# Thirteen gate/up units of a gated mix kernel as seven-product 2x2 blocks, with the operand sums and the normaliser work moved around them

## The chip, the cores and the metric

The kernel runs on one core of one Trainium2 chip. The metric is the device time of one execution in microseconds (us); it is compared by runs of both kernels on the same chip, in rounds. A single run on one core is called slow when it is over 1.5% above the fastest run of the same kernel.

Engines in the profile: PE is the matmul engine (TensorE), PEld its weight loads, DVE is VectorE, ACT ScalarE, POOL GpSimd, SP the engine that issues most DMAs.

## The reference, cut to what matters

```python
def _B_ref(x, w_gate, w_up, w_down):              # D = 640, F = 1728, S = 2048, bf16
    return (_gelu(x @ w_gate) * (x @ w_up)) @ w_down

g = _sigmoid((x * gate_w).sum(-1, keepdims=True))
a = _A_ref(x, A_wqkv, A_wo)                       # linear attention with 32 heads of 20
b = _B_ref(x, B_w_gate, B_w_up, B_w_down)
return g * a + (1 - g) * b
```

The attention part divides by a normaliser, `den` below; its input is also x.

## The kernel before

The 2048 tokens are worked in four quarters of 512. Per quarter there is a gate/up stage ("E"): 13 full f-tiles of 128 hidden columns and one half tile, which holds gate and up for the last 64 columns. A full f-tile is two groups of five matmuls of 512 columns, one group for gate and one for up. E of quarter q is followed by the output stage ("F") of quarter q-1, and the last quarter's F ends the kernel. Before all that, quarter 0 has its E stage and a stage "KQ" makes keys and queries. In the F stage a "join" is the DVE instruction that combines a finished PSUM bank with a stored partial result and so frees the bank.

The F stage already multiplies 2x2 blocks with 7 products in place of 8 (the Strassen-Winograd scheme), from sums of blocks that VectorE prepares ("S sums", `phase_S`, of tokens; "T sums", of weights). PSUM has eight banks, handed out in turn.

```python
    def ps_tile(name, hold=False):                 # eight banks, in turn
        b = bank_at[0] % NB
        ...
        return banks[:, b * QW : (b + 1) * QW]

    def e_mm(ps, w, ft, q, t0=0, tw=QW):           # QW = 512, ND = 5
        for dk in range(ND):
            nc.tensor.matmul(ps[:, t0 : t0 + tw], lhsT=w[:, dk, ft * P : (ft + 1) * P],
                             rhs=xT[q][:, dk, t0 : t0 + tw], start=(dk == 0), stop=(dk == ND - 1))

    def e_out(q, ft, psg, psu):
        gl = work.tile([P, QW], BF16, name="gl")
        nc.scalar.activation(out=gl[:], in_=psg[:], func=ACT.Gelu_apprx_tanh)
        nc.vector.scalar_tensor_tensor(out=hT_cur[q][:, ft, :], in0=psu[:], scalar=HS, in1=gl[:],
                                       op0=ALU.mult, op1=ALU.mult)

    def phase_E(q, ft):
        if ft < NF - 1:
            psg = ps_tile("ps_g")
            e_mm(psg, wg, ft, q)
            psu = ps_tile("ps_u")
            e_mm(psu, wu, ft, q)
            e_out(q, ft, psg, psu)
        ...                                        # the half tile
    ...
    side.update({                                  # what is queued behind which unit
        ...
        (2, 0): [(den_inv, 6), (den_out, 6, 7)],
        (2, 2): [(s_tiles, 1), (phase_S, 1, "h", 0)],
        (2, 3): [(phase_S, 1, "h", 1)],
        (2, 4): [(phase_S, 1, "p"), (phase_S, 1, "x")],
        (2, 5): [(den_mul, 8, 9)],
        (2, 7): [(den_inv, 8), (den_mul, 10, 11), (den_out, 8, 9)],
        ...
    })
    with tc.manual_schedule():                     # every engine runs in the order written
        for q in range(1, NQ):
            for ft in range(q == 1, NF):
                phase_E(q, ft)
                beside(q, ft)
            phase_F(q - 1)
        phase_F(NQ - 1)
```

`den_mul` (POOL) multiplies 640 columns, `den_inv` (DVE) reduces and inverts, `den_out` (POOL, then a transposing DMA) scales. `(2, 5)` means: in quarter 2 (the third), behind the unit at place 5. `("F", q, a)`, `("C", q, a)` and `("D", q, a)` are places in half a of the F stage of quarter q.

Of the kernel before, what the change touches and what calls it, by code (L numbers as in the profile page):

```python
# [8 lines left out]
ACT = mybir.ActivationFunctionType  # L9
ALU = mybir.AluOpType  # L10
# [6 lines left out]
def kernel(  # L17
# [48 lines left out]
    ov = ctx.enter_context(tc.tile_pool(name="ov", bufs=1))  # L66
    work = ctx.enter_context(tc.tile_pool(name="work", bufs=3))
    psum = ctx.enter_context(tc.tile_pool(name="psum", bufs=1, space=bass.MemoryType.PSUM))
    NB = 8
# [19 lines left out]
    x_sb = [x_all[:, 4 * q : 4 * q + 4, :] for q in range(NQ)]  # L89
    pk_q = [ov.tile([P, 4, D], BF16, name=f"pk{q}", tag="slab_a", bufs=NQ) for q in range(NQ)]  # L90
    pk = [pk_q[t // 4][:, t % 4, :] for t in range(NT)]
    WQK = 2 * D + 1
# [91 lines left out]
    def e_mm(ps, w, ft, q, t0=0, tw=QW):  # L184
# [3 lines that stand above are left out]
# [6 lines left out]

    def phase_E(q, ft):
        if ft < NF - 1:
            psg = ps_tile("ps_g")
            e_mm(psg, wg, ft, q)
            psu = ps_tile("ps_u")
            e_mm(psu, wu, ft, q)  # L200
            e_out(q, ft, psg, psu)
        else:
            pgu = ps_tile("ps_gu")
            e_mm(pgu, wgu, 0, q)
            gl = work.tile([P, QW], BF16, name="gl")
            nc.scalar.activation(out=gl[0:FL, :], in_=pgu[0:FL, :], func=ACT.Gelu_apprx_tanh)
            nc.vector.scalar_tensor_tensor(out=hT_cur[q][0:FL, ft, :], in0=pgu[FL:P, :], scalar=HS,
                                           in1=gl[0:FL, :], op0=ALU.mult, op1=ALU.mult)

    def h_twin(q):  # L210
# [95 lines left out]

    g_sb = ov.tile([P, ND, D], BF16, name="g_sb", tag="slab_g")

# [253 lines left out]

    def phase_S(q, part, a=None):
        lo, hi = PART[part]
        c0, c1 = (0, TW) if a is None else (a * P, a * P + P)

        def blk(i, k):
            return ktiles(part, k, hT_cur[q], pqT[q])[:, :, i * TW + c0 : i * TW + c1]

        s1, s2, s3, s4 = (SS[q, i][:, lo:hi, c0:c1] for i in range(1, 5))  # L570
        sums(s3, blk(0, 0), blk(1, 0), ALU.subtract)
        sums(s1, blk(1, 0), blk(1, 1), ALU.add)
        sums(s2, s1, blk(0, 0), ALU.subtract)
        sums(s4, blk(0, 1), s2, ALU.subtract)

    side = {}

    def beside(*key):
# [3 lines left out]
    def phase_F(q):  # L582
# [34 lines left out]
        for a in range(2):  # L617
# [30 lines left out]
            d = keep_slot("d")  # L648
            join(d[:], b22, 0, c2)
            beside("D", q, a)  # L650
            product(x, a, 3, 0, 0, 3, 0, 0, False, True)
# [27 lines left out]
    with tc.manual_schedule():  # L679
        for ft in range(3, NF):  # L680
            phase_E(0, ft)
            if ft in (8, 9, 10, 11):
                x_sums((3, 1, 2, 4)[ft - 8])
        g4 = [banks[:, b * QW : (b + 1) * QW] for b in (6, 7)]
        g_done = 0
# [37 lines left out]
    def t_tiles():  # L723
        TS[2] = ov.tile([P, KS, HALF], FP16, name="t2", tag="slab_e")

    def m_part(i):
        phase_M(((0, 0), (0, 1), (1, 0)) if i == 0 else ((1, 1), (2, 0), (2, 1)))
# [15 lines left out]
        (1, 11): [(phase_S, 0, "x", 0)],  # L743
        ("F", 0, 0): [(phase_S, 0, "h", 1)],
        ("D", 0, 0): [(phase_S, 0, "p", 1), (phase_S, 0, "x", 1)],
        ("F", 0, 1): [(den_mul, 4, 5)],
        ("D", 0, 1): [(den_inv, 4), (den_mul, 6, 7), (den_out, 4, 5)],
        (2, 0): [(den_inv, 6), (den_out, 6, 7)],
        (2, 2): [(s_tiles, 1), (phase_S, 1, "h", 0)],
        (2, 3): [(phase_S, 1, "h", 1)],  # L750
        (2, 4): [(phase_S, 1, "p"), (phase_S, 1, "x")],
        (2, 5): [(den_mul, 8, 9)],
        (2, 7): [(den_inv, 8), (den_mul, 10, 11), (den_out, 8, 9)],
        (2, 9): [(den_inv, 10), (den_out, 10, 11)],
        (3, 0): [(den_mul, 12, 13)],
        (3, 2): [(den_inv, 12), (den_mul, 14, 15), (den_out, 12, 13)],
        (3, 4): [(den_inv, 14), (den_out, 14, 15)],
        (3, 5): [(s_tiles, 2), (phase_S, 2, "h", 0)],
        (3, 6): [(phase_S, 2, "h", 1)],
        (3, 7): [(phase_S, 2, "p"), (phase_S, 2, "x")],  # L760
        ("F", 2, 0): [(s_tiles, 3), (phase_S, 3, "h", 0)],
        ("D", 2, 0): [(phase_S, 3, "p", 0)],
        ("F", 2, 1): [(phase_S, 3, "x", 0), (phase_S, 3, "h", 1)],
        ("D", 2, 1): [(phase_S, 3, "p", 1)],
        ("F", 3, 0): [(phase_S, 3, "x", 1)],
    })
    with tc.manual_schedule():
        for q in range(1, NQ):
            for ft in range(q == 1, NF):
                phase_E(q, ft)  # L770
                beside(q, ft)
            phase_F(q - 1)
        phase_F(NQ - 1)
# [27 lines left out]
```

## Time and profile before

| | before |
|---|---|
| time, first six runs | 265.31 us (265.06 to 265.51) |
| span of the profiled run | 263.8 us |
| PE / DVE / ACT / POOL busy | 98 / 70 / 36 / 19% |
| one plain gate/up unit on PE | 2.16 us |
| E stage of the third and fourth quarter | 29.14 us each |
| F stage | 17.87 us |

From the page of the kernel before: busy time of each engine, then the busy tenths of PE and its granted clock (tenths of full speed) in 40 equal slices of the span.

```profile
PE 259.1 (98%) x1587; PEld 144.9 (55%) x1587; DVE 184.7 (70%) x343; ACT 94.5 (36%) x187; POOL 50.2 (19%) x50
PE   8999999999999999999999999999999999999994
PEclk9999999999999999999999999999999999999999
```

From 11.8 us on, when the first loads have landed, PE never pauses, and its clock is never lowered. A busy PE can still hide waits, so the next view matters more: the chain of work that ended last, in order of time (start us, us, what). Five of its pieces, from the third quarter's E stage to the start of the fourth's; L186 is gate/up, L603 and L610 the F stage:

```profile
148.25 29.14 PE banks L186 x135
177.39 7.33 PE banks L603 x54
184.72 0.65 PE banks L610 x8
185.37 9.89 PE banks L603 x72
195.26 29.14 PE banks L186 x135
```

Each piece starts where the one before ends, and each is PE. 29.14 us / 135 = 0.2159 us a matmul: PE streams 512 columns after 512 columns and waits for nobody. So only less work on PE can shorten this stretch; this change takes the streamed columns.

What do the others do meanwhile? The table by stage of the kernel before (window, length, then busy time of PE, PEld, DVE, ACT, POOL, the granted clock, DMA share and GB/s), for the same two E stages:

```profile
148.25:177.40 29.15, 29.15 (x137) 13.23 (x136) 26.20 (x44) 7.77 (x13) 16.37 (x13) 1.00 0.21 46
195.30:224.40 29.10, 29.10 (x137) 13.24 (x136) 22.30 (x38) 7.76 (x13) 8.04 (x6) 1.00 0.15 34
```

ACT has room; DVE is at 90% in the third quarter. Part of that is not work but waiting: DVE and POOL hold each other up. In order of time, DVE first, then POOL (start us, us, engine, line, operation, what, shape):

```profile
156.49 1.76 DVE L61 TENSOR_TENSOR s_1_1577<-hb 128x768 f16<-128x768 bf16 x1
158.29 1.64 DVE L61 TENSOR_TENSOR s_2_1578<-s_1_1577,hb 128x768 f16<-128x768 f16 x1
159.96 0.56 DVE L61 TENSOR_TENSOR sp<-hb,s_2_1578 128x768 f16<-128x768 bf16 x1
156.11 3.40 POOL L510 TENSOR_TENSOR prod<-pq_91,zrep 128x640 f32<-128x640 bf16 x2
```

The same kind of sum of 768 columns takes 1.76 and 1.64 us while POOL multiplies, and 0.56 us once POOL has stopped. The Trainium skill says the same in "SBUF — State Buffer", § Who interferes with whom: a VectorE instruction with two SBUF inputs contends with a GpSimd instruction that reads SBUF, one with at most one SBUF input, outside what the page calls two-port modes, does not.

The cost of a matmul of about half width can be read from this kernel too. Groups of instructions, shapes kept apart (what, shape, count, busy us and mean ns, idle before):

```profile
L249 PEld LDWEIGHTS <-xT_86 128*128 128x128 bf16 x60 | 5.9, 98 | 5.3
L249 PE MATMUL banks<-wqk,xT_86 128*128 128x257 bf16 x20 | 2.9, 273 | 0.0
```

The 273 ns include the depth of the pipeline; the pace is the difference of starts. The chain has a KQ tile, ten 512- and five 257-column matmuls, at 2.71 us; ten at 0.216 us are 2.16, so the five take 0.55 us, 110 ns each. The weight load of 98 ns fits under that.

### The profile page before, as it was taken

The numbers are of one execution on the slowest core, as the hardware profiler recorded it, in microseconds if no ns is written. First come the engines' busy times: TensorE is split into PE (matmuls) and PEld (weight loads), VectorE is DVE, ScalarE is ACT, GpSimd is POOL, SyncE is SP. The second block draws the span as 40 slices with busy tenths as digits, with TensorE's granted clock in tenths as the row PEclk, the third lists the DMA queues.
The fourth block names the chain that finished last, engine by engine and source line by source line (L and its number), as shares of the span: only waits on it lengthen the run. The fifth ranks groups of instructions, "written<-read, shape, count | busy, mean of one in ns | idle before, by whom it ended". The sixth has DMA issues, their size and how long they took to land.

```text
span 263.8 us, 4180 instructions
## 1 busy us (share of the span) xinstructions
PE 259.1 (98%) x1587; PEld 144.9 (55%) x1587; DVE 184.7 (70%) x343; ACT 94.5 (36%) x187; POOL 50.2 (19%) x50
## 2 busy tenths in 40 slices
PE   8999999999999999999999999999999999999994
PEld 3644444555556775444567544446764444767672
DVE  0775358589889995799994889982335997676132
ACT  3688222744555234822321122223112222312110
POOL 5000000000000004684000761383001810000000
PEclk9999999999999999999999999999999999999999
DMA  7999999000000019125001050031110220011011
GB/s 228 291 301 267 210 320 249 6 0 2 0 0 2 0 35 316 51 71 107 0 0 52 13 135 3 0 65 39 50 50 2 50 50 0 2 50 41 13 50 50
DMA packets 34959, 20.91 MB, mean 79 GB/s; under 512 B 20732, under 2 KB 34940, under 8 KB 34940
## 3 DMA queue, kind: packets, MB, share of 16 engines
q1 hardware_dynamic: 34498, 20.16, 28.2%
q10 hardware_dynamic: 442, 0.49, 0.6%
q8 instruction: 12, 0.20, 0.3%
q14 instruction: 7, 0.06, 0.1%
HBM read 12.62 MB, written 2.62 MB: 58 GB/s over the span
## 4 chain that ended last, share of the span: by engine, by line
PE 94%; DMA 4%; DVE 0%; SPq 0%; issue 0%
PE banks L186 44%; PE banks L603 26%; PE banks L249 14%; PE banks L347 6%; DMA wqk<-in_A_wqkv_dram 3%; PE banks L338 2%; DMA x_all<-in_A_x_dram 1%; PE banks L610 1%; PE banks L478 0%; PE banks L447 0%; DVE o_out L629 0%; SPq L122 0%; PE banks L417 0%
## 5 line engine op out<-in xcount | busy, mean ns | idle before, releaser
L191 ACT ACTIVATE gl<-banks 128x512 bf16<-128x512 f32 x52 | 31.0, 598 | 74.6 <-PE banks L186 70.6
L186 PEld LDWEIGHTS <-wu 128*128 128x128 bf16 x260 | 25.4, 98 | 30.7
L186 PEld LDWEIGHTS <-wg 128*128 128x128 bf16 x260 | 25.2, 98 | 29.4 <-issue 0.5
L192 DVE SCALAR_TENSOR_TENSOR hT_148<-banks,gl 128x512 bf16<-128x512 f32 x26 | 17.4, 681 | 11.4 <-PE banks L186 10.2
L192 DVE SCALAR_TENSOR_TENSOR hb<-banks,gl 128x512 bf16<-128x512 f32 x26 | 17.4, 677 | 10.9 <-PE banks L186 8.7
L266 ACT ACTIVATE phi<-banks 128x512 bf16<-128x512 f32 (+1 forms) x36 | 18.7, 526 | 15.5 <-ACT eneg L267 6.3
L510 POOL TENSOR_TENSOR prod<-pq_89,zrep 128x640 f32<-128x640 bf16 x2 | 2.8, 1408 | 95.0 <-ACT zrep L418 95.0
L625 ACT ACTIVATE m_all<-banks,omg_s 128x320 f32<-128x320 f32 x16 | 8.4, 528 | 27.2 <-PE banks L603 27.2
L629 DVE SCALAR_TENSOR_TENSOR o_out<-banks,omg_s,m_all 128x320 bf16<-128x320 f32 x24 | 12.2, 542 | 5.9 <-PE banks L603 5.9
L186 PE MATMUL banks<-xT_86,wg 128*128 128x512 bf16 x65 | 16.2, 379 | 0.0
L186 PE MATMUL banks<-xT_87,wg 128*128 128x512 bf16 x65 | 16.2, 379 | 0.0
L186 PE MATMUL banks<-xT_85,wg 128*128 128x512 bf16 x65 | 16.1, 379 | 0.0
L186 PE MATMUL banks<-xT_85,wu 128*128 128x512 bf16 x65 | 16.1, 379 | 0.0
L186 PE MATMUL banks<-xT_86,wu 128*128 128x512 bf16 x65 | 16.1, 379 | 0.0
L186 PE MATMUL banks<-xT_87,wu 128*128 128x512 bf16 x65 | 16.1, 379 | 0.0
L186 PE MATMUL banks<-xT_88,wg 128*128 128x512 bf16 x65 | 16.1, 379 | 0.0
L186 PE MATMUL banks<-xT_88,wu 128*128 128x512 bf16 x65 | 16.1, 379 | 0.0
L629 DVE SCALAR_TENSOR_TENSOR m_all<-banks,omg_s,m_all 128x320 f32<-128x320 f32 x8 | 4.4, 551 | 14.6 <-PE banks L603 14.5
L249 PE MATMUL banks<-wqk,xT_85 128*128 128x512 bf16 (+2 forms) x80 | 12.4, 304 | 0.1
L510 POOL TENSOR_TENSOR prod<-pq_90,zrep 128x640 f32<-128x640 bf16 x4 | 7.4, 1862 | 24.4 <-DVE den L516 24.4
L629 DVE SCALAR_TENSOR_TENSOR o_out<-banks,omg_s,sw 128x320 bf16<-128x320 f32 x8 | 4.4, 549 | 10.7 <-PE banks L603 5.6
L625 ACT ACTIVATE sw<-banks,omg_s 128x320 f32<-128x320 f32 x8 | 4.2, 527 | 20.6 <-PE banks L603 20.6
(216 smaller groups left out, 470.0 us busy)
## 6 DMA issues: line engine op xcount, KB each, us to landing
out_dram<-o_out SPq DMA_DIRECT2D x16, 160.0 KB, 1.8
wd<-in_B_w_down_dram SPq DMA_DIRECT2D x1, 2080.0 KB
x_all<-in_A_x_dram SPq DMA_DIRECT2D x3, 640.0 KB, 6.1
wqk<-in_A_wqkv_dram SPq DMA_DIRECT2D x1, 800.0 KB
wg<-in_B_w_gate_dram SPq DMA_DIRECT2D x1, 800.0 KB, 9.2
wu<-in_B_w_up_dram SPq DMA_DIRECT2D x1, 800.0 KB
wv<-in_A_wqkv_dram SPq DMA_DIRECT2D x1, 800.0 KB
wo_g<-in_A_wo_dram SPq DMA_DIRECT2D x2, 375.0 KB
```

What stands on the lines that cost most here:

```text
L186: nc.tensor.matmul(ps[:, t0 : t0 + tw], lhsT=w[:, dk, ft * P : (ft + 1) * P], rhs=xT[q][:, dk, t0 : t0 + tw], start=(dk == 0), stop=(dk == ...
L191: nc.scalar.activation(out=gl[:], in_=psg[:], func=ACT.Gelu_apprx_tanh)
L192: nc.vector.scalar_tensor_tensor(out=hT_cur[q][:, ft, :], in0=psu[:], scalar=HS, in1=gl[:], op0=ALU.mult, op1=ALU.mult)
L249: nc.tensor.matmul(ps[:, 0 : hi - lo], lhsT=xT[q][:, dk, sl * P : (sl + 1) * P], rhs=wqk[:, dk, lo:hi], start=(dk == 0), stop=(dk == ND - 1),)
L266: nc.scalar.activation(out=e[:, lo:top], in_=ps[:, lo:top], func=ACT.Exp)
L338: nc.tensor.matmul(gp[:, 0:HALF], lhsT=x_all[:, st, (ND - 1) * P : ND * P], rhs=pk[st][:, j * HALF : (j + 1) * HALF], start=(st == 0), sto ...
L347: nc.tensor.matmul(bank[:, 0:HALF], lhsT=lhsT, rhs=rhs, start=(start and n == 0), stop=(stop and n == NG2 - 1), skip_group_check=True)
L510: nc.gpsimd.tensor_tensor(out=prod[:], in0=pq[st][:], in1=zrep[:], op=ALU.mult)
L603: nc.tensor.matmul(bank[:, 0:HALF], lhsT=lhs(sa, ia, ka * KS + kk, a), rhs=rhs(sb, kb * KS + kk, jb), start=(start and kk == 0), stop=(sto ...
L610: nc.tensor.matmul(bank[:, 0:HALF], lhsT=lhsT, rhs=wd[r : r + FL, NF - 1, j * HALF : (j + 1) * HALF], start=st_, stop=not a, skip_group_ch ...
L625: nc.scalar.activation(out=c[:], in_=bank[:, 0:HALF], func=ACT.Copy, scale=omg[i])
L629: nc.vector.scalar_tensor_tensor(out=out, in0=bank[:, 0:HALF], scalar=omg[i], in1=c[:], op0=ALU.mult, op1=ALU.add)
```

## The change

Its intent is to stream fewer columns. In 13 of the 26 full units of the last two quarters, four of the five k-tiles are taken as two pairs (k = 0, 1). With j the half of the token columns, the unit computes

G_j = g0 X0j + g1 X1j and U_j = u0 X0j + u1 X1j,

eight block products, from seven: P1 = g0 X00, g1 X10, S1 T1, S2 T2, S3 T3, S4 X11, u1 T4, with S1 = u0+u1, S2 = S1-g0, S3 = g0-u0, S4 = g1-S2 and T1 = X01-X00, T2 = X11-T1, T3 = X11-X01, T4 = X10-T2. Then G_0 = P1 + g1 X10, G_1 = P1 + S2 T2 + S1 T1 + S4 X11, and both U halves share P1 + S2 T2 + S3 T3. The fifth k-tile stays plain. (The letters are the other way round from the F stage: here S are sums of weights and T of tokens.) The weight sums (S, and s5 = g - u of the fifth k-tile, nine blocks in all) are made early on POOL, which has nothing to do then, written to DRAM (the stash) and fetched back, one unit's worth at a time, into a ring of two slots. The token sums (T) are made once a quarter.

The order changes as well: the half tile comes first, the new units (a minus sign in `runs`) stand in pairs with a plain unit between, the first product of the next unit is issued early, the S sums for the F stage are spread between the pairs, and the den work moves mostly into the F stages. There POOL is held behind a join (`pool_hold`, a copy of one column of the join's result), so that it does not multiply while DVE makes S sums. The diff, cut to its core:

```diff
+    WF = tuple(range(4, 12))                       # the eight f-tiles with stored sums
+    WS = 2 * 4 + 1
...
+    def w_sums(i):                                 # on POOL, two f-tiles at a time
+        ...
+            nc.gpsimd.tensor_tensor(out=out, in0=a0, in1=a1, op=op)
+    def w_fetch(*keys, eng=dma):                   # ring of two slots
+        ...
+            slot = ew["ring"][ew["m"] % 2]
+            eng(out=slot, in_=stash[WF.index(ft)])
...
+    def ew_first(q, ft):
+        x = ps_tile("ps_wx")
+        cg = ew["cg"][ew["n"] % 3]
+        ew_mm(x[:, lo_h], 2, <wg, tiles 0-1>, <xT lo half>, True, True)                  # P1
+        nc.scalar.copy(out=cg[:, lo_h], in_=x[:, lo_h])
+
+    def phase_EW(q, ft, early, fetch):
+        ub, gb = ps_tile("ps_wu"), ps_tile("ps_wg")
+        ew_mm(ub, 1, wt(wu, 4), xt(4, slice(0, QW)), True)
+        ew_mm(ub[:, lo_h], 2, wt(wu, 2), t_(4))
+        ew_mm(gb[:, lo_h], 1, wt(wg, 4), xt(4, lo_h), True)
+        ew_mm(gb[:, hi_h], 1, s_(5), xt(4, hi_h))
+        ew_mm(x[:, lo_h], 2, s_(2), t_(2), False, True)
+        nc.scalar.copy(out=cg[:, hi_h], in_=x[:, lo_h])
+        early()                                     # P1 of the next unit
+        ew_mm(gb[:, lo_h], 2, wt(wg, 2), xt(2, lo_h))
+        ew_mm(ub[:, hi_h], 2, s_(1), t_(1), False, True)
+        ew_mm(gb[:, hi_h], 2, s_(4), xt(2, hi_h), False, True)
+        ew_mm(x[:, lo_h], 2, s_(3), t_(3), False, True)
+        ut = work.tile([P, 2, HT], FP32, name="ut", tag="prod", bufs=2)
+        nc.vector.tensor_tensor(out=cg[:, hi_h], in0=ub[:, hi_h], in1=cg[:, hi_h], op=ALU.add)
+        nc.scalar.activation(out=ut[:, 1], in_=x[:, lo_h], func=ACT.Copy, scale=HS)
+        w_fetch(*fetch, eng=dma2)                   # issued by ACT, for the unit after the next
+        ew_finish()                                 # GELU and product of the unit before
+        nc.vector.tensor_tensor(out=cg, in0=gb, in1=cg, op=ALU.add)
+        nc.vector.scalar_tensor_tensor(out=ut[:], in0=<ub>, scalar=HS, in1=<ut[:, 1]>, ...)
+        def finish():
+            nc.scalar.activation(out=gl[:], in_=cg, func=ACT.Gelu_apprx_tanh)
+            nc.gpsimd.tensor_tensor(out=hT_cur[q][:, ft, :], in0=<ut>, in1=gl[:], op=ALU.mult)
+        ew["open"].append(finish)
...
+        ("F", 1, 0): [(phase_S, 1, "h", 1, (2, 4)), (phase_S, 1, "p", 1), (phase_S, 1, "x", 1)],
+        ("D", 1, 0): [(pool_hold,), (den_mul, 10, 11)],
+        ("F", 1, 1): [(den_inv, 10), (den_mul, 12, 13), (den_out, 10, 11)],
...
+    runs = {
+        1: list(range(1, NF)),
+        2: [13, 0, 1, -4, -5, 2, -6, -7, 3, -8, -9, 12, -10, 11],
+        3: [13, 0, 1, 2, -4, -5, 3, -6, -7, 12, -8, -9, 10, 11],
+    }
...
+            ew_finish()
             phase_F(q - 1)
```

More of the change, by code (lines that the diff above doesn't have):

```diff
@@ L67 @@
     work = ctx.enter_context(tc.tile_pool(name="work", bufs=3))
+    dram = ctx.enter_context(tc.tile_pool(name="dram", bufs=1, space=bass.MemoryType.DRAM))
     psum = ctx.enter_context(tc.tile_pool(name="psum", bufs=1, space=bass.MemoryType.PSUM))
@@ L89, with pk_tiles @@
     x_sb = [x_all[:, 4 * q : 4 * q + 4, :] for q in range(NQ)]
-    pk_q = [ov.tile([P, 4, D], BF16, name=f"pk{q}", tag="slab_a", bufs=NQ) for q in range(NQ)]
-    pk = [pk_q[t // 4][:, t % 4, :] for t in range(NT)]
+    WF = tuple(range(4, 12))
+    WS = 2 * 4 + 1
+    ws = [ov.tile([P, 2, WS, P], FP16, name=f"ws{i}", tag="slab_a", bufs=NQ) for i in range(3)]
+    ws.append(ov.tile([P, 2, WS, P], FP16, name="ws3", tag="slab_g"))
+    pk_q = []
+    pk = {}
+    def pk_tiles(qs):
+        for q in qs:
+            pk_q.append(ov.tile([P, 4, D], BF16, name=f"pk{q}", tag="slab_a", bufs=NQ))
+            for t in range(4):
+                pk[4 * q + t] = pk_q[q][:, t, :]
+    pk_tiles((0,))
     WQK = 2 * D + 1
@@ L193, in e_out, with phase_E @@
                                        op0=ALU.mult, op1=ALU.mult)
-    def phase_E(q, ft):
+    def phase_E(q, ft, early=None):
         if ft < NF - 1:
@@ L198, in phase_E @@
             e_mm(psg, wg, ft, q)
+            if early:
+                early()
+                ew_finish()
             psu = ps_tile("ps_u")
@@ L204, in phase_E @@
             e_mm(pgu, wgu, 0, q)
+            if early:
+                early()
+                ew_finish()
             gl = work.tile([P, QW], BF16, name="gl")
@@ L208, in phase_E @@
                                            in1=gl[0:FL, :], op0=ALU.mult, op1=ALU.mult)
+    stash = dram.tile([len(WF), P, WS, P], FP16, name="stash")
+    def w_sums(i):
+        f0 = WF[2 * i] * P
+        g, u = (w[:, :, f0 : f0 + 2 * P].rearrange("p k (f c) -> p f k c", f=2) for w in (wg, wu))
+        o = ws[i]
+        s1, s2, s3, s4 = (o[:, :, 2 * n : 2 * n + 2, :] for n in range(4))
+        for out, a0, a1, op in ((s1, u[:, :, 0:2, :], u[:, :, 2:4, :], ALU.add), (s2, s1, g[:, :, 0:2, :], ALU.subtract),
+                                (s3, g[:, :, 0:2, :], u[:, :, 0:2, :], ALU.subtract),
+                                (s4, g[:, :, 2:4, :], s2, ALU.subtract),
+                                (o[:, :, 8:9, :], g[:, :, 4:5, :], u[:, :, 4:5, :], ALU.subtract)):
+            nc.gpsimd.tensor_tensor(out=out, in0=a0, in1=a1, op=op)
@@ new lines, in w_stash, with x_tiles, t_sums, blk @@
+    def w_stash(i):
+        for f in range(2):
+            dma(out=stash[2 * i + f], in_=ws[i][:, f])
+    HT = QW // 2
+    ew = {}
+    def x_tiles():
+        tx = big.tile([P, 4, 2, HT], FP16, name="tx", tag="pq", bufs=NQ)
+        ew["tx"] = [tx[:, n] for n in range(4)]
+    def t_sums(q):
+        def blk(k, j):
+            return xT[q][:, 2 * k : 2 * k + 2, j * HT : (j + 1) * HT]
+        t1, t2, t3, t4 = ew["tx"]
+        for out, a0, a1 in ((t1, blk(0, 1), blk(0, 0)), (t2, blk(1, 1), t1), (t3, blk(1, 1), blk(0, 1)),
+                            (t4, blk(1, 0), t2)):
+            sums(out, a0, a1, ALU.subtract)
@@ new lines, in ew_tiles @@
+    def ew_tiles():
+        cg = big.tile([P, 2, QW], FP32, name="cg", tag="pq", bufs=NQ)
+        ew["cg"] = [cg[:, 0], cg[:, 1], zacc[:, 0:QW]]
+        ew["n"] = 2
+        ew["first"] = {}
+        ew["open"] = []
+    def w_fetch(*keys, eng=dma):
+        if "ring" not in ew:
+            wr = big.tile([P, 2, WS, P], FP16, name="wr", tag="xT", bufs=NQ - 1)
+            ew["ring"] = [wr[:, 0], wr[:, 1]]
+            ew["m"] = 0
+            ew["at"] = {}
+        for q, ft in keys:
+            slot = ew["ring"][ew["m"] % 2]
+            ew["m"] += 1
+            eng(out=slot, in_=stash[WF.index(ft)])
+            ew["at"][q, ft] = slot
@@ new lines, in ew_finish, with ew_mm @@
+    def ew_finish():
+        for f in ew.get("open", ()):
+            f()
+        ew["open"] = []
+    lo_h, hi_h = slice(0, HT), slice(HT, QW)
+    def ew_mm(out, k, lhs, rhs, start=False, stop=False):
+        for n in range(k):
+            nc.tensor.matmul(out, lhsT=lhs(n), rhs=rhs(n), start=start and n == 0, stop=stop and n == k - 1,
+                             skip_group_check=True)
+    def ew_first(q, ft):
+        x = ps_tile("ps_wx")
+        cg = ew["cg"][ew["n"] % 3]
+        ew["n"] += 1
+        ew_mm(x[:, lo_h], 2, lambda n: wg[:, n, ft * P : (ft + 1) * P], lambda n: xT[q][:, n, lo_h], True, True)
+        nc.scalar.copy(out=cg[:, lo_h], in_=x[:, lo_h])
+        ew["first"][q, ft] = x, cg
@@ new lines, in phase_EW, with wt, xt, s_ @@
+    def phase_EW(q, ft, early, fetch):
+        fs = slice(ft * P, (ft + 1) * P)
+        sw_ = ew["at"][q, ft]
+        if (q, ft) not in ew["first"]:
+            ew_first(q, ft)
+        x, cg = ew["first"][q, ft]
+        def wt(w, k0):
+            return lambda n: w[:, k0 + n, fs]
+        def xt(k0, c):
+            return lambda n: xT[q][:, k0 + n, c]
+        def s_(i):
+            return lambda n: sw_[:, 2 * (i - 1) + n, :]
+        def t_(i):
+            return lambda n: ew["tx"][i - 1][:, n, :]
+        ub, gb = ps_tile("ps_wu"), ps_tile("ps_wg")
[5 more added lines that the diff above has]
+        nc.scalar.copy(out=cg[:, hi_h], in_=x[:, lo_h])
+        early()
+        ew_mm(gb[:, lo_h], 2, wt(wg, 2), xt(2, lo_h))
[6 more added lines that the diff above has]
+        w_fetch(*fetch, eng=dma2)
+        ew_finish()
+        nc.vector.tensor_tensor(out=cg, in0=gb, in1=cg, op=ALU.add)
+        nc.vector.scalar_tensor_tensor(out=ut[:], in0=ub.rearrange("p (j c) -> p j c", j=2), scalar=HS,
+                                       in1=ut[:, 1:2].to_broadcast([P, 2, HT]), op0=ALU.mult, op1=ALU.add)
+        def finish():
+            gl = work.tile([P, QW], BF16, name="gl")
+            nc.scalar.activation(out=gl[:], in_=cg, func=ACT.Gelu_apprx_tanh)
+            nc.gpsimd.tensor_tensor(out=hT_cur[q][:, ft, :], in0=ut[:].rearrange("p j c -> p (j c)"), in1=gl[:],
+                                    op=ALU.mult)
+        ew["open"].append(finish)
@@ L305, in k_first @@
         held.clear()
-    g_sb = ov.tile([P, ND, D], BF16, name="g_sb", tag="slab_g")
     def x_blk(i, k):
@@ L561, with phase_S @@
     TW = 2 * P
-    def phase_S(q, part, a=None):
+    def phase_S(q, part, a=None, which=(3, 1, 2, 4)):
         lo, hi = PART[part]
@@ L568, in blk @@
             return ktiles(part, k, hT_cur[q], pqT[q])[:, :, i * TW + c0 : i * TW + c1]
-        s1, s2, s3, s4 = (SS[q, i][:, lo:hi, c0:c1] for i in range(1, 5))
-        sums(s3, blk(0, 0), blk(1, 0), ALU.subtract)
-        sums(s1, blk(1, 0), blk(1, 1), ALU.add)
-        sums(s2, s1, blk(0, 0), ALU.subtract)
-        sums(s4, blk(0, 1), s2, ALU.subtract)
+        s = {i: SS[q, i][:, lo:hi, c0:c1] for i in range(1, 5)}
+        for i in which:
+            a0, a1, op = {3: (blk(0, 0), blk(1, 0), ALU.subtract), 1: (blk(1, 0), blk(1, 1), ALU.add),
+                          2: (s[1], blk(0, 0), ALU.subtract), 4: (blk(0, 1), s[2], ALU.subtract)}[i]
+            sums(s[i], a0, a1, op)
     side = {}
+    last_d = [None]
     def beside(*key):
@@ L649, in phase_F @@
             join(d[:], b22, 0, c2)
+            last_d[0] = d
             beside("D", q, a)
@@ L681 @@
             phase_E(0, ft)
+            if ft == 5:
+                for i in range(len(ws)):
+                    w_sums(i)
             if ft in (8, 9, 10, 11):
                 x_sums((3, 1, 2, 4)[ft - 8])
+        for i in range(len(ws)):
+            w_stash(i)
+        pk_tiles((1, 2, 3))
+        g_sb = ov.tile([P, ND, D], BF16, name="g_sb", tag="slab_g")
         g4 = [banks[:, b * QW : (b + 1) * QW] for b in (6, 7)]
@@ L724, in t_tiles, with pool_hold @@
         TS[2] = ov.tile([P, KS, HALF], FP16, name="t2", tag="slab_e")
+    def pool_hold():
+        h = work.tile([P, 1], FP32, name="hold", bufs=1)
+        nc.gpsimd.tensor_copy(out=h[:], in_=last_d[0][:, 0:1])
     def m_part(i):
@@ L743 @@
         (1, 11): [(phase_S, 0, "x", 0)],
-        ("F", 0, 0): [(phase_S, 0, "h", 1)],
+        (1, 12): [(den_mul, 4, 5)],
+        ("F", 0, 0): [(w_fetch, (2, 4), (2, 5)), (phase_S, 0, "h", 1)],
         ("D", 0, 0): [(phase_S, 0, "p", 1), (phase_S, 0, "x", 1)],
-        ("F", 0, 1): [(den_mul, 4, 5)],
-        ("D", 0, 1): [(den_inv, 4), (den_mul, 6, 7), (den_out, 4, 5)],
-        (2, 0): [(den_inv, 6), (den_out, 6, 7)],
-        (2, 2): [(s_tiles, 1), (phase_S, 1, "h", 0)],
-        (2, 3): [(phase_S, 1, "h", 1)],
@@ L751 @@
-        (2, 4): [(phase_S, 1, "p"), (phase_S, 1, "x")],
-        (2, 5): [(den_mul, 8, 9)],
-        (2, 7): [(den_inv, 8), (den_mul, 10, 11), (den_out, 8, 9)],
-        (2, 9): [(den_inv, 10), (den_out, 10, 11)],
-        (3, 0): [(den_mul, 12, 13)],
-        (3, 2): [(den_inv, 12), (den_mul, 14, 15), (den_out, 12, 13)],
-        (3, 4): [(den_inv, 14), (den_out, 14, 15)],
-        (3, 5): [(s_tiles, 2), (phase_S, 2, "h", 0)],
-        (3, 6): [(phase_S, 2, "h", 1)],
-        (3, 7): [(phase_S, 2, "p"), (phase_S, 2, "x")],
@@ L761 @@
-        ("F", 2, 0): [(s_tiles, 3), (phase_S, 3, "h", 0)],
-        ("D", 2, 0): [(phase_S, 3, "p", 0)],
-        ("F", 2, 1): [(phase_S, 3, "x", 0), (phase_S, 3, "h", 1)],
-        ("D", 2, 1): [(phase_S, 3, "p", 1)],
-        ("F", 3, 0): [(phase_S, 3, "x", 1)],
-    })
+        ("F", 0, 1): [(x_tiles,), (t_sums, 2), (den_inv, 4), (den_mul, 6, 7), (den_out, 4, 5)],
+        ("D", 0, 1): [(den_inv, 6), (den_out, 6, 7)],
+        (2, 0): [(ew_tiles,), (s_tiles, 1), (den_mul, 8, 9)],
+        (2, 1): [(den_inv, 8), (den_out, 8, 9)],
@@ new lines @@
+        ("F", 1, 0): [(phase_S, 1, "h", 1, (2, 4)), (phase_S, 1, "p", 1), (phase_S, 1, "x", 1)],
+        ("D", 1, 0): [(pool_hold,), (den_mul, 10, 11)],
+        ("F", 1, 1): [(den_inv, 10), (den_mul, 12, 13), (den_out, 10, 11)],
+        ("D", 1, 1): [(den_inv, 12), (den_mul, 14, 15), (den_out, 12, 13)],
+        (3, 0): [(t_sums, 3), (s_tiles, 2)],
+        (3, 1): [(den_inv, 14), (den_out, 14, 15)],
+        ("F", 2, 0): [(phase_S, 2, "h", 1, (2, 4))],
+        ("D", 2, 0): [(phase_S, 2, "p", 1), (phase_S, 2, "x", 1), (s_tiles, 3)],
@@ new lines @@
+        ("F", 2, 1): [(phase_S, 3, "h", 0)],
+        ("D", 2, 1): [(phase_S, 3, "p", 0), (phase_S, 3, "x", 0)],
+        ("F", 3, 0): [(phase_S, 3, "h", 1)],
+        ("D", 3, 0): [(phase_S, 3, "p", 1), (phase_S, 3, "x", 1)],
+    })
+    for q, n in ((1, 4), (2, 5)):
+        for k, work_ in ((0, ("h", 0, (3,))), (1, ("h", 0, (1, 2))), (3, ("h", 0, (4,))), (4, ("p", 0, (3, 1))),
+                         (6, ("p", 0, (2, 4))), (7, ("x", 0)), (9, ("h", 1, (3, 1)))):
+            side.setdefault((q + 1, min(n + k, NF - 1)), []).append((phase_S, q, *work_))
@@ L767 @@
+    runs = {
[3 more added lines that the diff above has]
+    }
+    wins = [(q, -ft) for q in runs for ft in runs[q] if ft < 0]
     with tc.manual_schedule():
         for q in range(1, NQ):
-            for ft in range(q == 1, NF):
-                phase_E(q, ft)
-                beside(q, ft)
+            for n, ft in enumerate(runs[q]):
+                nxt = runs[q][n + 1] if n + 1 < len(runs[q]) else 0
+                early = (lambda f=-nxt: ew_first(q, f)) if nxt < 0 else (lambda: None)
+                if ft < 0:
+                    k = wins.index((q, -ft)) + 2
+                    phase_EW(q, -ft, early, wins[k : k + 1])
+                else:
+                    phase_E(q, ft, early if q > 1 else None)
+                beside(q, n + (q == 1))
+            ew_finish()
```

## The prediction

> **What bounds it now.** TensorE. The page gives PE 98% of a 263.8 us span at full granted clock; the chain that ended last is 94% PE, and from 11.8 to 260.2 us, in order of time, it is matmuls without a gap. A plain gate/up unit (10 matmuls of 512 columns) takes 2.16 us, 216 ns a matmul; a quarter's 27 groups take 29.1 us (stage table, 148.25 to 177.4 and 195.3 to 224.4). In those stages DVE is busy 26.2 and 22.3 us, ACT 7.8 each, POOL 16.4 and 8.0. So only fewer streamed columns shorten the kernel.
>
> **Removed.** In 13 units, two of the five k-pairs become 7 instead of 8 block products. The new unit streams one 512-column and sixteen 256-column matmuls: 4608 columns for 5120. A 256-column matmul I cost from the trace: a KQ tile of ten 512- and five 257-column matmuls takes 2.71 us, so 257 columns take 110 ns (the Trainium skill, "TensorE: Matmul & The Clock Gate", Back-to-back issue gap, has 262 cycles for 256; the trace agrees). Unit: 0.216 + 16 x 0.109 = 1.96 us, a gain of 0.195 us; 13 units: 2.5 us, all of it on the critical path. Weight loads stay hidden (98 ns each in the groups view, below 109). This is a ceiling of about 1%.
>
> **Added, off the path unless it runs late.**
> - DVE: per new unit 256- and 512-column adds and a 512-column multiply-add from PSUM, 0.4 + 0.67 + 0.68 = 1.75 us for 0.68. ACT: three 256-column copies (about 0.38 each), GELU 0.60, a DMA issue of 0.4: 2.1 us for 0.6. POOL: one 512-column multiply, about 1.1 us (1.4 for 640 columns).
> - In a cycle of two new units and a plain one (6.08 us) DVE has 4.2 + S sums 1.1 to 1.7, ACT about 5, POOL 2.3. They fit, narrowly: all eight banks are used once per cycle. The tightest spot is the second unit of a pair: the scaled copy and the DMA issue come before the copy that the third product waits for; I find 0.1 to 0.3 us of slack.
> - S sums beside POOL work: in the DVE timeline at 156 to 160 us 768-column sums took 1.1 to 1.8 us while POOL ran, 0.55 otherwise, as the exclusive lock in the skill's "SBUF - State Buffer" would have it. The moved den work and the hold lessen this in the F stages.
> - Weight sums on POOL (idle from 8 to 103 us), about 5 us per pair, 20 us; they may slow the x sums. Stash: 2.4 MB written after loads that keep the queues full to about 46 us. The first KQ writes to reused buffers come at 51 us, where DVE has about 0.5 us of slack: I expect 0 to 1 us of stall here.
> - Fetches of 295 KB, needed about 4.5 us after the slot comes free; I estimate 3 to 4 us from the landing times (160 KB in 1.8 us).
>
> **Sum.** 265.3 - 2.5 + about 0.7 of new stalls (KQ start 0.4, pairs 0.3) = 263.4 us; 262.6 to 265.0 should hold it 8 times in 10. Faster by over 2%: 0.01; within 2%: 0.95; slower by over 2%: 0.04.
>
> **Right if** the new units take 1.96 us on PE, both quarters' stages shrink to about 27.7 and 27.9 us, F stages stay at 17.9, and KQ starts at most a microsecond late. **Wrong if** PE idles before third products (waiting for ACT), before the fetched sums (DMA), or for banks behind a DVE backlog in the pairs; if 16-bit sums mixed with bf16 stream slower than 110 ns; or if the stash delays KQ by more than a microsecond.

## The result, and the profile after

| | before | after |
|---|---|---|
| time, median | 265.39 us (20 runs, 264.95 to 266.66) | 262.94 us (10 runs, 262.20 to 266.38) |
| span of the profiled run | 263.8 us | 261.1 us |
| E stage, third / fourth quarter | 29.14 / 29.14 us | 27.77 / 27.96 us |
| F stages | 17.87 us | 17.87 to 17.89 us |

The ratio of the fast runs is 0.990, with a 95% interval of 0.9886 to 0.9915. Ratios here are the mean time of one kernel's fast runs over that of the other's of the same rounds, so not quite the ratio of the medians quoted. One run of ten, 266.38 us at a mean clock of 0.991, counted as slow and is not in the ratio. By the 2% measure the kernels are the same; the gain is 1% and clear of the noise.

The page of the kernel after, the line of busy times:

```profile
PE 256.5 (98%) x1678; PEld 153.8 (59%) x1678; DVE 206.1 (79%) x393; ACT 107.9 (41%) x226; POOL 88.0 (34%) x84
```

PE is as full as before with 91 more matmuls (13 units, 17 for 10) and 2.6 us less busy time. The others took on 21, 13 and 38 us. The table by stage of the kernel after, the same two E stages:

```profile
148.31:176.08 27.77, 27.77 (x187) 18.03 (x185) 24.26 (x47) 14.42 (x33) 14.97 (x12) 1.00 0.49 118
193.95:221.91 27.96, 27.96 (x179) 17.36 (x178) 26.38 (x47) 14.38 (x32) 13.43 (x11) 1.00 0.34 80
```

PE's busy time equals the length of the stage in both. The third quarter lost 1.37 us with seven new units, the fourth 1.18 us with six: 0.196 and 0.197 us a unit. One cycle of a pair in the chain of work after (L199 plain, L290 new units):

```profile
157.63 1.08 PE banks L199 x5
158.71 0.22 PE banks L290 x2
158.93 1.08 PE banks L199 x5
160.01 3.71 PE banks L290 x32
163.72 1.08 PE banks L199 x5
```

Two new units are the 34 matmuls of L290: 3.71 + 0.22 = 3.93 us, 1.96 us each, against 2.16 for a plain one. In the piece of 32 there are two of 512 columns; (3.71 - 2 x 0.216) / 30 = 109 ns for 256 columns, whether the operands are bf16, f16 or one of each. The pieces follow without a gap.

How close it is shows on ACT. The lines of ACT in order of time in the second unit of the first pair after, then PE's third product that uses the copied bank again:

```profile
155.93 0.38 ACT L334 ACTIVATE ut<-banks 128x256 f32<-128x256 f32 x1 [0.45 <-PE banks L290]
155.93 0.36 ACTq L278 DMA_DIRECT2D wr<-stash  x1
156.80 0.37 ACT L326 COPY cg<-banks 128x256 f32<-128x256 f32 x1 [0.49 <-PE banks L290]
157.25 0.38 PE L290 MATMUL banks<-tx,wr 128*128 128x256 f16 x2
```

The copy at 156.80 ends at 157.17 us and the product that must not overwrite its source starts at 157.25: 0.08 us. But ACT had been idle for 0.49 us before the copy, waiting for PE. So the copy cannot come earlier, and ACT can lose about half a microsecond before PE notices.

Early in the kernel, POOL makes the weight sums from 19.6 to 42.4 us. DVE's x sums (2048 columns) meet its last two there: first DVE, then POOL in order of time:

```profile
37.61 2.17 DVE L61 TENSOR_TENSOR sx<-x_all 128x2048 f16<-128x2048 bf16 x1
42.40 1.21 DVE L61 TENSOR_TENSOR sx<-sx,x_all 128x2048 f16<-128x2048 f16 x1
38.66 2.13 POOL L240 TENSOR_TENSOR ws_80<-wg,ws_80 128x512 f16<-128x512 bf16 x1
```

Two of the four x sums stretch (2.17 and 1.57 us against 1.22), then DVE catches up: its first KQ instruction starts at 49.94 us, at 49.88 before. From the start of KQ to the first unit of the second quarter it is 52.06 us in both kernels (46.55 to 98.61, 46.61 to 98.67). Nothing was lost here.

### The profile page after: what moved, and what is told of

It is laid out like the page before. It is cut to its first block, busy times and chain, and to the rows that moved or that the text cites. A ratio compares the mean times of both kernels' runs of the same rounds, so it can differ in the third digit from the quotient of the medians.

```text
span 261.1 us, 4562 instructions
## 1 busy us (share of the span) xinstructions
PE 256.5 (98%) x1678; PEld 153.8 (59%) x1678; DVE 206.1 (79%) x393; ACT 107.9 (41%) x226; POOL 88.0 (34%) x84
## 4 chain that ended last, share of the span: by engine, by line
PE 96%; DMA 3%; DVE 0%; issue 0%
PE banks L199 34%; PE banks L742 26%; PE banks L388 16%; PE banks L290 10%; PE banks L485 6%; DMA x_all<-in_A_x_dram 3%; PE banks L476 2%; PE banks L749 1%; PE banks L616 0%; PE banks L585 0%; PE banks L190 0%; DVE o_out L768 0%; PE banks L555 0%
## 5 line engine op out<-in xcount | busy, mean ns | idle before, releaser
L204 ACT ACTIVATE gl<-banks 128x512 bf16<-128x512 f32 x39 | 23.2, 596 | 34.7 <-PE banks L199 31.5
L199 PEld LDWEIGHTS <-wu 128*128 128x128 bf16 x195 | 19.1, 98 | 21.5
L199 PEld LDWEIGHTS <-wg 128*128 128x128 bf16 x195 | 18.8, 98 | 20.5 <-issue 0.5
L764 ACT ACTIVATE m_all<-banks,omg_s 128x320 f32<-128x320 f32 x16 | 8.4, 527 | 27.3 <-PE banks L742 27.2
L199 PE MATMUL banks<-xT_89,wg 128*128 128x512 bf16 x65 | 16.2, 379 | 0.0
L199 PE MATMUL banks<-xT_89,wu 128*128 128x512 bf16 x65 | 16.2, 379 | 0.0
L199 PE MATMUL banks<-xT_88,wg 128*128 128x512 bf16 x65 | 16.1, 379 | 0.0
L199 PE MATMUL banks<-xT_88,wu 128*128 128x512 bf16 x65 | 16.1, 379 | 0.0
L290 PE MATMUL banks<-tx,wr 128*128 128x256 f16 x78 | 14.9, 273 | 0.0
L768 DVE SCALAR_TENSOR_TENSOR o_out<-banks,omg_s,m_all 128x320 bf16<-128x320 f32 x24 | 12.0, 536 | 3.1 <-PE banks L742 3.1
L764 ACT ACTIVATE sw<-banks,omg_s 128x320 f32<-128x320 f32 x8 | 4.2, 527 | 21.0 <-PE banks L742 21.0
L290 PEld LDWEIGHTS <-wr 128*128 128x128 f16 x117 | 11.4, 98 | 1.3
L344 POOL TENSOR_TENSOR hT_151<-ut,gl 128x512 bf16<-128x512 f32 x7 | 8.4, 1207 | 10.9 <-ACT gl L343 7.2
L654 DVE TENSOR_REDUCE den<-prod 128x32 f32<-128x640 f32 x14 | 10.9, 811 | 1.3 <-POOL prod L648 1.3
L388 PE MATMUL banks<-wqk,xT_89 128*128 128x512 bf16 (+1 forms) x60 | 11.5, 344 | 0.0
L388 PE MATMUL banks<-wqk,xT_91 128*128 128x512 bf16 (+1 forms) x60 | 11.5, 344 | 0.0
```

The costliest lines, as they stand in the source:

```text
L290: nc.tensor.matmul(out, lhsT=lhs(n), rhs=rhs(n), start=start and n == 0, stop=stop and n == k - 1, skip_group_check=True)
L388: nc.tensor.matmul(ps[:, 0 : hi - lo], lhsT=xT[q][:, dk, sl * P : (sl + 1) * P], rhs=wqk[:, dk, lo:hi], start=(dk == 0), stop=(dk == ND - 1),)
L654: nc.vector.tensor_reduce(out=den[:, i, :], in_=dn[st + i][:].rearrange("p (h c) -> p h c", c=Dh), axis=AX.X, op=ALU.add)
L764: nc.scalar.activation(out=c[:], in_=bank[:, 0:HALF], func=ACT.Copy, scale=omg[i])
L768: nc.vector.scalar_tensor_tensor(out=out, in0=bank[:, 0:HALF], scalar=omg[i], in1=c[:], op0=ALU.mult, op1=ALU.add)
```

## The experiments

All are edits of the kernel after, and all gave correct results. Kernels are compared only within the same rounds. Theory: the gain is the streamed columns and nothing else, and the rest of the change only makes room. Rivals: part of the gain comes from the moved work; or the room was there anyway and the moves are idle. By the 2% measure every run but that of experiment 4 is the same as the kernel before; the differences told below are smaller, and where the intervals of two ratios overlap they rest on the stages in the traces.

### 1. The moves alone

```diff
-        2: [13, 0, 1, -4, -5, 2, -6, -7, 3, -8, -9, 12, -10, 11],
-        3: [13, 0, 1, 2, -4, -5, 3, -6, -7, 12, -8, -9, 10, 11],
+        2: [13, 0, 1, 4, 5, 2, 6, 7, 3, 8, 9, 12, 10, 11],
+        3: [13, 0, 1, 2, 4, 5, 3, 6, 7, 12, 8, 9, 10, 11],
     # and: no w_sums, w_stash, w_fetch, t_sums
```

> The change's new order of den and S work and the hold stay, but all 13 new units are plain ones again, with no weight sums, stash, fetches or moving-operand sums. Theory A (the whole gain is fewer columns on TensorE): TensorE has no gaps here either, both quarters take 29.1 us again, ratio to the kernel before 0.998 to 1.002. Rival B (part of the gain comes from the moved den and S work): ratio 0.997 or lower.

Measured: 265.29 us, ratio 0.998 (0.995 to 1.0017). The two E stages in the table by stage (columns as before):

```profile
148.35:177.49 29.14, 28.98 (x135) 13.22 (x136) 15.24 (x31) 8.36 (x14) 7.16 (x6) 1.00 0.22 38
195.36:224.50 29.14, 28.98 (x134) 13.22 (x136) 16.02 (x33) 8.35 (x14) 5.75 (x5) 1.00 0.18 36
```

They are as long as before, and PE's list of waits has nothing there. (The busy time of PE falls 0.16 us short of the length because a few matmul records are missing from this trace: its chain has 132 of the 135 of a stage.) The moves by themselves gain nothing: the interval alone would allow a gain of over 1 us, the stages do not.

### 2. New units in the third quarter only

```diff
-        3: [13, 0, 1, 2, -4, -5, 3, -6, -7, 12, -8, -9, 10, 11],
+        3: [13, 0, 1, 2, 4, 5, 3, 6, 7, 12, 8, 9, 10, 11],
     # and: no t_sums of the fourth quarter
```

> Only the seven new units of the third quarter stay. Theory A: 7 x 0.195 = 1.4 us off, so about 264.0 us, ratio 0.995 (0.994 to 0.996); third quarter's stage 27.8 us, fourth 29.1. Rival B or any fixed cost of weight sums and stash: more than 264.4 us.

Measured: 264.06 us, ratio 0.994 (0.9903 to 0.9977). The same two stages:

```profile
148.57:176.34 27.77, 27.56 (x183) 18.02 (x185) 24.27 (x47) 14.33 (x33) 14.96 (x12) 1.00 0.41 100
194.21:223.34 29.13, 28.97 (x134) 13.23 (x136) 16.02 (x33) 8.36 (x14) 5.75 (x5) 1.00 0.17 36
```

The gain goes with the number of units, and storing the sums carries no visible fixed cost. The interval of the ratio is wide, so this rests on the stages.

### 3. Without the hold on POOL

```diff
-        ("D", 1, 0): [(pool_hold,), (den_mul, 10, 11)],
+        ("D", 1, 0): [(den_mul, 10, 11)],
```

> The whole change without the hold that keeps POOL's den products behind a join of the second output stage. Theory A (slack is large in the output stages: the S sums of the second half end 5 us before their first use): no TensorE gap, ratio 0.990 as with the change, though 128- to 768-column S sums at 178 to 183 us stretch to 1 us and more. Rival C (the hold is needed): the stretched sums and joins come late, TensorE waits 0.5 us or more in that stage, ratio 0.992 or higher.

Measured: 264.25 us, ratio 0.993 (0.9898 to 0.9967). The expectation failed and the rival holds: this F stage takes 19.46 us in place of 17.87. In order of time, DVE, POOL and PE of this run:

```profile
178.13 1.77 DVE L61 TENSOR_TENSOR s<-hb 128x768 f16<-128x768 bf16 x1
179.93 1.32 DVE L61 TENSOR_TENSOR hdiff<-hb 64x128 f16<-64x128 bf16 x1
184.19 0.54 DVE L768 SCALAR_TENSOR_TENSOR m_all<-banks,omg_s,m_all 128x320 f32<-128x320 f32 x1
177.73 3.43 POOL L648 TENSOR_TENSOR prod<-pq,zrep 128x640 f32<-128x640 bf16 x2
184.79 0.43 PE L749 MATMUL banks<-wd,hb 64*128 64x320 bf16 x3 [1.42 <-DVE m_all L768]
```

Beside POOL's products one S sum takes 1.77 us (0.55 with the hold) and a 128-column difference 1.32 (0.22). What I had overlooked is not the first use of the sums but the queue: a join (L768) stands behind them on DVE, and PE needs the bank that it frees. It starts at 184.19 us here, 8.39 us after the stage's start, with the hold at 182.16, 6.08 us after it. So the hold is worth 1.6 us on the stage, more than half of the change's gain. The whole times, of different rounds, differ by 1.3 us, and the two intervals overlap; the stage is what shows it.

### 4. Den work between the pairs

```diff
-        (2, 1): [(den_inv, 8), (den_out, 8, 9)],
+        (2, 5): [(den_mul, 8, 9), (den_inv, 8), (den_out, 8, 9)],
+        (2, 8): [(den_mul, 10, 11), (den_inv, 10), (den_out, 10, 11)],
     # and: (den_mul, 8, 9) off (2, 0); the work of 12 to 15 moved one place earlier in the F stage
```

> The whole change, but the den work of token tiles 8 to 11 (products on POOL, reductions and reciprocal on VectorE, scaling on POOL) stands between the unit pairs of the third quarter; that of tiles 12 to 15 takes the freed places. Theory A2 (the moves are what makes room: VectorE is idle only 3.5 us of this quarter's 27.8): VectorE waits about 2.8 us for the products and works 2.6 us twice, TensorE waits 1 to 4 us in this quarter, 264 to 267 us. Rival: the eight banks absorb it, no gap, 262.9 us.

Measured: 271.78 us, ratio 1.024 (1.0205 to 1.0281): slower than before the change. The quarter takes 36.15 us, 8.4 more than in the change; I had expected 1 to 4. Waits of PE in this run (who waited for whom, us in total, times, longest):

```profile
PE banks L290 <- DVE ut L338: 2.9, 2, 2.3
PE banks L290 <- ACT cg L326: 2.5, 2, 1.8
PE banks L290 <- ACT zacc L326: 2.0, 2, 1.1
```

The chain of work runs POOL `prod`, DVE `den`, `dtmp`, `rg`, then S sums, `cg`, `ut`. The products and `ut` share two buffers (tag "prod" in the diff), so ACT's next scaled copy waited for the reductions as well: ACT waited 2.21 us for `den` at 163.59 us. How much is the DVE queue and how much the shared buffers can't be told apart in this run, and no run had separate buffers.

### 5. The seven units in a row

```diff
-        2: [13, 0, 1, -4, -5, 2, -6, -7, 3, -8, -9, 12, -10, 11],
+        2: [13, 0, 1, 2, 3, 12, -4, -5, -6, -7, -8, -9, -10, 11],
```

> In the third quarter the seven new units stand in a row instead of in pairs with plain units between; number of units as in the change. Theory A2 (pairs are needed): fetches land 2.7 us after issue but only 2.5 us lie between a slot's last read and its next use, so TensorE waits about 0.3 to 1 us a unit from the third on; VectorE, 1.75 us a unit of 1.96, also can't take S sums between; together 1 to 5 us longer than the change, 264 to 268 us. Rival: no gap, 262.9 us.

Measured: 264.66 us, ratio 0.997 (0.9955 to 0.9994); the quarter takes 29.79 us, 2.0 more than in pairs. In order of time, PE in the third unit of the row:

```profile
164.21 0.27 PE L290 MATMUL banks<-xT,wg 128*128 128x256 bf16 x1
164.95 0.28 PE L290 MATMUL banks<-xT,wr 128*128 128x256 bf16 x1 [0.47 <-DMA wr<-stash]
```

PE stops at the first matmul that reads the fetched sums (`wr`). In the third, fifth, sixth and seventh unit it comes 0.29 to 0.63 us later after the unit's start than the 0.54 us of an undisturbed unit, 2.0 us in all; the 0.47 us in the line is less because the modelled end of a matmul lies behind its pace. The fetch lands 2.8 us after its issue, and in a row only one unit lies between a slot's last read and its next use. DVE, which I suspected too, is busy 24.5 of 29.8 us and is not in PE's list of waits. So in this order it is mostly the DMA that needs the plain unit between pairs. Not all: ACT issues the first fetches 0.12 us after the slot's last read, those of the sixth and seventh unit 0.44 and 0.22 us after it, because its scaled copy just before had to wait until POOL's product freed a `ut` buffer. About 0.4 us of the 2.0 may belong to that (an estimate from these starts; no run separates the two).

### 6. One and two more copies on ACT in each new unit

```diff
         w_fetch(*fetch, eng=dma2)
+        for r in range(1):          # 2 in the other run
+            nc.scalar.copy(out=zsum[:, 0:256], in_=zsum[:, 320:576])
```

> One more 256-column copy on ScalarE (onto a tile that is no longer read, about 0.37 us) in each new unit, behind the fetch's issue. In the trace of the change ScalarE is idle 0.43 to 0.5 us before the copy that the third product of a pair's second unit waits for, and that copy ends 0.08 us before the product starts. Theory: the added 0.37 us fits into the idle time: no gap of more than 0.1 us a unit, 262.9 to 263.4 us. Rival (slack of 0.1 us or less): 0.3 us in each of 6 units, 264.7 us.

> Two more 256-column copies on ScalarE in each new unit, 0.74 us. Theory (0.5 us of slack before the copy, 0.08 us behind it): TensorE waits 0.1 to 0.2 us in each second unit, and as ScalarE then has about 6.2 us to do in a cycle of 6.08 us, up to 0.2 us more a cycle: 1 to 3 us in all, 264 to 266 us. Rival: 262.9 us, the copies hide.

Measured: with one, 262.81 us, ratio 0.990 (0.9876 to 0.9917), no wait. With two, 264.51 us, ratio 0.996 (0.9945 to 0.9981), E stages 28.64 and 28.77 us, 0.87 and 0.81 us longer, and PE waits at the third product of the second units for ACT's copy. A copy adds 0.42 us to ACT's queue, so ACT's slack lies between 0.42 and 0.84 us, as its idle time of 0.43 to 0.5 us said.

### 7. All sixteen units that the stash allows

```diff
-        2: [13, 0, 1, -4, -5, 2, -6, -7, 3, -8, -9, 12, -10, 11],
-        3: [13, 0, 1, 2, -4, -5, 3, -6, -7, 12, -8, -9, 10, 11],
+        2: [13, 0, 1, -4, -5, 2, -6, -7, 3, -8, -9, 12, -10, -11],
+        3: [13, 0, 1, -4, -5, 2, -6, -7, 3, -8, -9, 12, -10, -11],
```

> All eight stashed tiles as new units in both quarters: 16 units in place of 13. Theory A with room to spare: 3 x 0.195 = 0.6 us less, 262.4 us, ratio 0.988. Rival D (VectorE is full): its busy time in the fourth quarter, 26.4 us of 28.0, would rise by 2 x 1.07 to 28.5 us of 27.6, so banks come free late and TensorE waits 0.5 to 2 us in the fourth quarter or at the start of the output stage behind it; 262.5 to 264.5 us.

Measured: 264.22 us, ratio 0.994 (0.99 to 0.9977). Both E stages shrink to 27.57 us, as predicted by the columns, and both give it back in the F stage behind: the first takes 18.71 us for 17.87. ACT and then PE in order of time, at the start of that stage:

```profile
178.00 0.63 ACT L343 ACTIVATE gl<-cg 128x512 bf16<-128x512 f32 x1 [0.80 <-DVE cg L337]
178.54 0.51 ACT L764 ACTIVATE sw<-banks,omg_s 128x320 f32<-128x320 f32 x1
179.10 0.30 PE L742 MATMUL banks<-t,s 128*128 128x320 f16 x1 [0.68 <-ACT sw L764]
```

The F stage's third product may not overwrite its bank before ACT has copied it (L764). The bank's product had ended at about 177.2, but in front of it in ACT's queue stood the GELU of the last new unit, which waited 0.80 us for DVE. In the fourth quarter DVE was late, not full: it is busy 24.35 of 27.57 us, idle 0.64 us or more three times, and my sum of 28.5 us was too high. In the third quarter its total, 24.08 us, misleads: from 154.5 us to beyond this wait its longest idle time is 0.18 us, so there it was full. Part of that is POOL again, DVE first, then POOL:

```profile
171.36 1.14 DVE L61 TENSOR_TENSOR s<-s,pqT 128x256 f16<-128x256 f16 x1
172.53 1.13 DVE L61 TENSOR_TENSOR sp<-pqT,s 128x256 f16<-128x256 bf16 x1
171.19 2.32 POOL L344 TENSOR_TENSOR hT<-ut,gl 128x512 bf16<-128x512 f32 x2 [3.55 <-PE banks L290]
```

Such sums of 256 columns take 0.29 us elsewhere; beside the new units' own products on POOL these two lose 1.7 us together, more than the wait. The change's trace has the same two (1.13 us each). Whether moving them would make room for sixteen units was not tried.

### 8. Sixteen and fifteen with that GELU queued later, sixteen begun earlier, and a control

```diff
         for q in range(1, NQ):
             ...
-            ew_finish()
             phase_F(q - 1)
...
-        ("C", 1, 0): [(h_twin, 2)],
+        ("C", 1, 0): [(h_twin, 2), (ew_finish,)],     # behind the copy; ("C", 2, 0) likewise
```

The two "late" runs and the control have this edit. The run begun earlier keeps the change's queue order and has, in both quarters, `[13, 0, -4, -5, 1, -6, -7, 2, -8, -9, 3, -10, -11, 12]`, with the S sums one and two places earlier to match.

> Sixteen new units as in the run of sixteen, but the GELU and the product of a quarter's last new unit are queued behind the output stage's first scaled copy (c1) in place of ahead of it. In the run of sixteen TensorE waited 0.7 us (and 0.8 us with its pipeline's end) at the third product of both output stages for c1, which stood on ScalarE behind that GELU, which waited for VectorE. Theory E (that queue order is the whole loss): no wait there, quarters 27.57 us, output stages 17.9, 16 x 0.195 = 3.1 us off, 262.3 us, ratio 0.988. Rival D (VectorE is full): the wait moves to the join of the output stage, 263 to 264.5 us.

> As the run before it with 8 units in the third quarter and 7 in the fourth. Theory E: 2.9 us off, 262.5 us, ratio 0.989. Rival D: no gain over the change, 263 us or more.

> Sixteen new units, first pair one place earlier, so that each quarter ends with a plain unit; queue order as in the change. Theory E: the plain unit takes up the lag, so 262.3 us, if the earlier start does not hurt. Rival: VectorE still has den work in the first units (its reductions end at 155.6 us in the change) and the early pair's adds wait behind it, so TensorE waits 0.5 us or more near the start of a quarter; 263 to 265 us.

> Control: the change's own 13 units with the last GELU queued behind c1. There was no wait at this place in the change, so both theories expect no change: 262.9 us, ratio 0.990.

| run | time, us | ratio (95%) | where PE waited, from the third quarter on |
|---|---|---|---|
| sixteen, late | 262.87 | 0.989 (0.9876 to 0.9912) | first F stage behind the units, 18.57 us |
| fifteen, late | 263.99 | 0.995 (0.9914 to 0.9992) | the same place, and a fetch |
| sixteen, early | 264.52 | 0.997 (0.9947 to 0.9994) | first units of both quarters |
| thirteen, late (control) | 263.00 | 0.991 (0.9885 to 0.9928) | nowhere |

The waits that set them back, from PE's lists of waits of three runs, one fence each: sixteen late (fifteen late has the same line), fifteen late, sixteen early:

```profile
PE banks L749 <- DVE m_all L768: 0.5, 1, 0.5
```

```profile
PE banks L290 <- DMA wr<-stash: 0.5, 1, 0.5
```

```profile
PE banks L290 <- DVE tx L61: 1.2, 1, 1.2
PE banks L290 <- ACT cg L298: 0.5, 1, 0.5
```

Before the third quarter, three of these four runs also wait 0.8 to 1.3 us for the first weights (`wqk`), ahead of all that the edits touch; it moves the later starts by up to 0.8 us, so stages are compared here and not start times.

Sixteen late: the wait for ACT is gone from both stages. The fourth quarter is then free of waits, 27.57 us and the first part of F 7.33 us as ever. In the F stage behind the third quarter the lag comes back at the next place, the join on DVE behind the S sums (as in experiment 3), and costs 0.7 us. From the start of the third quarter to the end of PE's work it takes 109.5 us (148.93 to 258.39), the change 109.4 (148.31 to 257.67): level, and so are the times. Theory E held for one quarter, the rival for the other.

Fifteen late: `-8, -9, -10` in its fourth quarter are three in a row, which I had not thought of, and the third waits for its fetch as in experiment 5. Its mean also has a run of 267.09 us in it. Sixteen early: the fourth quarter's first unit waits for the token sums (`tx`), in the third quarter a copy waits for a transposing DMA to free its buffer (the chain of work has POOL's `pq`, then DMA `pqT`, then ACT's copy). So the first three or four units of a quarter, in the change, are plain for a reason.

Eight units in the fourth quarter and seven in the third, with the late order, would by these stages take 27.57 + 27.77 us and no wait, 0.39 us less than the change (an estimate from the stages of two runs); that kernel was not run. None that was run beats the change clearly.

## Why the prediction was right, point by point

- *PE bounds the kernel, and only columns count*: right. The moves alone gave 0.998; seven of thirteen units gave 1.37 us on the stage.
- *A unit gains 0.195 us, 13 units 2.5 us*: right, 0.196 and 0.197 us a unit. The estimate from the 257-column matmuls of the kernel before was good to 1 ns.
- *F stages stay at 17.9 us*: right.
- *Added work a unit of 1.75 us on DVE, 2.1 on ACT, 1.1 on POOL*: right; the instructions of a new unit in the trace after add up to 1.79, 2.1 and 1.2 us.
- *About 0.7 us of new stalls*: this term was mis-sized; it measured 0. Of it, 0.4 us stood for a late KQ start: KQ and what follows it lasted 52.06 us as before; DVE had caught up, and its first write to the buffers that the stash had held came at 51.2 us in both kernels, with no idle time before it. The other 0.3 us stood for the pairs: PE's busy time equals the stage's length. I had put ACT's slack at 0.1 to 0.3 us; it is over 0.42 us, by the run with one more copy. That is why 262.94 us lies nearer to the sum without stalls (262.8) than to 263.4.
- *The moved den work and the hold lessen the contention*: right, and I gave it too little weight. Removing the hold alone costs about 1.6 us on the stage, and den work between the pairs 8.4 us. Their value was invisible in the comparison of before and after, where the F stage stays at 17.87 us.
- *Fetches land in 3 to 4 us, needed after 4.5*: they land in 2.7 us; from a slot's last read to its next use it is 4.5 us in the trace after (155.89 to 160.39 us). In a row it is a plain unit of 2.16 us less, and PE waits (experiment 5).

Not settled: how much of the stash's timing is slack. No run delayed it.

## What to carry to other kernels

When one engine is busy without a gap, count what it streams: the gain of a cheaper algorithm is then the columns saved times the pace, both readable from the trace before, and it is paid only if every other queue keeps its place. Judge added side work by what stands behind it in the same queue (a join, a copy that frees a bank), not by the first use of its own result; one GELU queued behind a copy in place of ahead of it was worth 0.7 us in one of two stages, and one engine's work held behind a join 1.6 us. A part of a change that shows no gain by itself can still be what the gain rests on, so undo the parts one at a time from the finished kernel too.

## What the Trainium skill lacked or had wrong

- "TensorE: Matmul & The Clock Gate", § Back-to-back issue gap, gives about 131 ns per matmul for a sustained stream of weight load and 512-column matmul and calls the longer figure that of an isolated one. Here the sustained stream takes 216 ns (29.14 us for 135), and 109 ns at 256 columns: the page's other formula (518 and 262 cycles), not its sustained one.
- The same page, § LDWEIGHTS, gives the number of columns divided by 1.2 in ns, 107 for 128; the records here have 98 ns, and 256-column matmuls at 109 ns with a new weight each are not slowed.
- I found on no page of it how operands of different 16-bit types stream; f16 weights with bf16 tokens, and bf16 weights with f16 tokens, took the same 109 ns.
- "DMA: Bandwidth & Descriptors", § Anatomy of one DMA, fits 2.0 us plus the bytes over 436 GB/s, for DMAs that POOL issues. The fetches here, issued by ACT, 288 KB, landed in 2.7 us, which that fit gives too; but the output DMAs of 160 KB, issued by SP, landed in 1.8 us, where it gives 2.4 (an estimate from the page's figures).
- "SBUF — State Buffer", § Who interferes with whom, agreed where it was looked for: sums with two SBUF inputs went from 0.55 to 1.77 us beside POOL. It has no word on what that does to the instructions queued behind; here it was 2.3 us for a join.
